# One decode step of attention and a feed-forward layer on one core: GpSimd issues the large loads in place of SP

## The chip, the cores and the metric

The kernel runs on one core of a Trainium2 chip. The metric is device time in microseconds. The engines are TensorE (PE), VectorE (DVE), ScalarE (ACT), GpSimd (POOL) and the sync engine (SP); transfers between HBM and the on-chip memory run on 16 DMA engines, whichever engine issues them.

## What is computed

One token's row x of 512 values is normalised; the result xn goes through grouped-query attention over a cache of 65536 positions (8 key heads, 4 query heads on each, 128 values a head) and through a feed-forward layer, and x and both are added.

```python
def _A_ref(x, k_cache, v_cache, wq, wo):
    q = (x @ wq) ...                        # 32 heads of 128
    scores = jnp.einsum("bhqd,bhkd->bhqk", q, k) * (Dh ** -0.5)
    p = _softmax(scores, axis=-1)
    o = jnp.einsum("bhqk,bhkd->bhqd", p, v)
    return o.reshape(B, Sq, Hq * Dh) @ wo   # heads brought together first
def _B_ref(x, w1, w2):
    return jnp.einsum("bsf,fd->bsd", jnp.maximum(x @ w1, 0), w2)   # 512 -> 1792 -> 512
xn = _layernorm(x, axis=-1)
return x + _A_ref(xn, ...) + _B_ref(xn, ...)
```

All data is float32. Keys and values are 268 MB each; wq and wo are 8.4 MB each, w1 and w2 3.7 MB each.

## The kernel before

The work is a chain of 34 turns on PE with the same code: a turn multiplies what lies in the key buffer kt by the current query columns (line 313). Turn 0 finds wq there and makes the queries; turns 1 to 32 find a chunk of keys (4 chunks of 16384 positions for each of 8 heads); the last finds wo. There is one key buffer kt and one value buffer vt, of 128 rows x 64 KB each; a chunk fills one. wt holds w1 and later w2.

Around a chunk: DVE transposes the scores (366) and finds the maximum (384 to 391). ACT takes the exponentials (254, 256); its first instruction also releases kt through the semaphore kfree. PE multiplies the probabilities by vt (292), and releases vt through vfree (299). `take(engine, semaphore, n)` waits until the semaphore has n and takes n off it. A transfer that lands raises its semaphore by 16: k or v for the chunks, on which PE waits.

SP issues all large transfers in one order: three pieces of wq into kt, w1 into wt, then in a loop values n on vfree and keys n+1 on kfree (lines 161 to 170), then wo in three pieces into kt, and, when the hidden row hT is there, w2 in five pieces into wt, and the store. ACT issues two loads of x (234, 235).

GpSimd prepares constants, finishes the norm (208 to 214), waits for w1 and multiplies it by xn and adds its four parts (219 to 224, whose end raises the semaphore sum); PE's line 281 sums that over the partitions, in every turn anew. GpSimd then waits until the last turn for the transposed row and makes hT (226). At the end PE adds w2's blocks (331, 339) as they land.

Of the kernel before, what the change touches and what calls it, by code (L numbers as in the profile page):

```python
# [13 lines left out]
D = 512  # L14
# [21 lines left out]
NCH = SK // CHUNK  # L36
# [6 lines left out]
WO_CUTS = [16, 8, 8]  # L43
W2_CUTS = [6, 4, 2, 1, 1]
# [5 lines left out]
def take(e, sem, n=1):  # L50

    return e.sem_inc(sem, -n).wait_op(sem, n, "sem-ge")  # L52


def starts(cuts):
    return [sum(cuts[:i]) for i in range(len(cuts) + 1)]

# [2 lines left out]
def attention_and_mlp_kernel(  # L60
# [12 lines left out]
    sp, pe, dve, act, pool = nc.sync, nc.tensor, nc.vector, nc.scalar, nc.gpsimd  # L73
    scale = float(DH) ** -0.5

    def sbuf(name, *shape):
        return nc.alloc_sbuf_tensor(name, list(shape), F32).ap()
# [3 lines left out]
    def sem(name):  # L81
        if name not in sems:
            sems[name] = nc.alloc_semaphore(name)
        return sems[name]

    def after(ins, name, n=1):

        return ins.wait_op(sem(name), n, "sem-ge")

    kt = sbuf("kt", P, CHUNK)  # L90
    vt = sbuf("vt", P, CHUNK)
    wt = sbuf("wt", P, FB * D)
# [20 lines left out]
    hT = sbuf("hT", P, FB)  # L113
# [25 lines left out]
    wo_row = wo[0].rearrange("d j n -> d (j n)")  # L139
    w1_row = w1.rearrange("p a f -> p (a f)")  # L140
    w2_row = w2.rearrange("p b n -> p (b n)")
    v_row = v[0].rearrange("(n p b) d -> n p (b d)", p=P, b=NB)
    wq_at, wo_at, w2_at = starts(WQ_CUTS), starts(WO_CUTS), starts(W2_CUTS)

    def of_own_row(cols, groups):
# [11 lines left out]
    for i in range(1, len(WQ_CUTS)):  # L157
        cut = slice(wq_at[i], wq_at[i + 1])
        sp.dma_start(kt[:, cut], wq_row[:, cut]).then_inc(sem(WQ_SEMS[i]), 16)  # L159
    sp.dma_start(wt, w1_row).then_inc(sem("w1"), 16)  # L160
    take(sp, sem("kfree"))
    sp.dma_start(kt, k[0, 0]).then_inc(sem("k"), 16)
    with sp.Fori(0, NCH - 1) as n:
        take(sp, sem("vfree"))
        sp.dma_start(vt, v_row[bass.ds(n, 1)].rearrange("o p n -> (o p) n")).then_inc(sem("v"), 16)
        take(sp, sem("kfree"))
        sp.dma_start(kt, k[0, bass.ds(n + 1, 1)].rearrange("o p n -> (o p) n")).then_inc(sem("k"), 16)
    take(sp, sem("vfree"))
    sp.dma_start(vt, v_row[NCH - 1]).then_inc(sem("v"), 16)
    take(sp, sem("kfree"))  # L170
    for i in range(len(WO_CUTS)):
        cut = slice(wo_at[i] * D, wo_at[i + 1] * D)
        sp.dma_start(kt[:, cut], wo_row[:, cut]).then_inc(sem(f"wo{i}" if i else "k"), 16)
    sp.wait_ge(sem("hT"), 1)
    for i in range(len(W2_CUTS)):
        cut = slice(w2_at[i] * D, w2_at[i + 1] * D)
        sp.dma_start(wt[:, cut], w2_row[:, cut]).then_inc(sem(f"w2{i}"), 16)  # L177
    sp.wait_ge(sem("y"), 1)
    sp.dma_start(out.rearrange("(p a) -> p a", p=P), ysb[:, 0, :]).then_inc(sem("ends"), 16)

# [3 lines left out]
    def link(ins):  # L184

        if chain[0]:
            after(ins, "pool", chain[0])
        chain[0] += 1
        return ins.then_inc(sem("pool"), 1)
# [22 lines left out]
    link(pool.tensor_scalar_mul(xn, xc, st[:, 7:8]))  # L212
    take(pool, sem("ends"), 16)
    after(pool.tensor_copy(qpad[:, :XA], xn), "pool", chain[0]).then_inc(sem("q"), 1)
    f = DFF_ALL
    w1_of = [wt[:, a * f : (a + 1) * f] for a in range(XA)]
    pool.wait_ge(sem("w1"), 16)
# [2 lines left out]
    last.then_inc(sem("pool"), 1)  # L220
    chain[0] += 1
    after(pool.tensor_add(w1_of[0], w1_of[0], w1_of[1]), "pool", chain[0])  # L222
    link(pool.tensor_add(w1_of[2], w1_of[2], w1_of[3]))  # L223
    after(pool.tensor_add(w1_of[0], w1_of[0], w1_of[2]), "pool", chain[0]).then_inc(sem("sum"), 1)  # L224
    hbig = ysum[:, : FB * 32].rearrange("p (b i) -> p b i", i=32)
    after(pool.tensor_scalar_max(hT, hbig[:, :, 0], 0.0), "hx").then_inc(sem("hT"), 1)  # L226


    def next_of(ins):
# [41 lines left out]
    with nc.body("turns", valid_engines=[pe.engine]):  # L271
# [3 lines left out]
        with pe.If(t > 1):  # L275
# [12 lines left out]
            n = NB // WIDE  # L288
# [167 lines left out]
```

## Time and profile before

| | us |
|---|---|
| median of 3 runs | 1303.71 |
| lowest and highest run | 1303.10 and 1303.74 |
| profiled execution: span from its first to its last instruction | 1301.3 |
| PE busy (matmul) | 774.9 |
| DVE busy | 274.8 |
| ACT busy | 76.2 |
| GpSimd busy | 34.8 |

Of the profiled execution the profile gives the span and no other time; the runs' median lies 2.4 us above it, which is taken for what lies around the span. The profile shows one execution. In its lines L313 is line 313 of the kernel, "kt<-k" is a tile written from a tensor, x31 a count. PEq, SPq and so on are the sequencers that issue. A transfer's time to landing runs from its issue to the semaphore. The timeline puts several like instructions of an engine together in one line, with the start of the first and their time in all, and behind them in brackets how long the engine was idle before.

### The profile page before, as it was taken

How to read it: one execution, taken by the hardware profiler on the slowest of the kernel's cores; microseconds unless marked ns; L12 is line 12 of the kernel's file. 1: busy time of each engine (PE TensorE's matmuls, PEld its weight loads, DVE VectorE, ACT ScalarE, POOL GpSimd, SP SyncE). 2: the span in 40 equal slices, each digit the busy share in tenths (PEclk: the TensorE clock that was granted, in tenths of full speed). 3: DMA queues.
4: the chain of work that ended last, by engine and by line, in shares of the span. 5: the costliest groups of instructions: out<-in, count | busy, mean ns of one | idle time of the engine just before them, and what ended most of it. 6: DMA issues, size and time to landing. Idle time of an engine off the chain costs nothing.

```text
span 1301.3 us, 13055 instructions
## 1 busy us (share of the span) xinstructions
PE 774.9 (60%) x5474; PEld 231.1 (18%) x5474; DVE 274.8 (21%) x466; ACT 76.2 (6%) x299; POOL 34.8 (3%) x30
## 2 busy tenths in 40 slices
PE   3365674665576456566555566666567466557557
PEld 1111121111121111121111121111112111112112
DVE  2211222211222220222220122221122221122222
ACT  1000000000000000000000000000000000000000
POOL 1900000000000000000000000000000000000000
PEclk9677877776887777786776777677777777777779
DMA  9999999999999999999999999999999999999998
GB/s 403 451 419 451 419 451 419 435 435 419 451 419 451 419 451 419 449 421 423 447 419 451 419 451 419 451 419 435 435 419 451 419 451 419 451 419 443 427 420 370
DMA packets 11236, 561.02 MB, mean 431 GB/s; under 512 B 1505, under 2 KB 1505, under 8 KB 1890
## 3 DMA queue, kind: packets, MB, share of 16 engines
q1 hardware_dynamic: 11088, 561.00, 99.7%
q10 hardware_dynamic: 146, 0.00, 0.0%
q8 instruction: 1, 0.02, 0.0%
q14 instruction: 1, 0.01, 0.0%
HBM read 560.99 MB, written 0.00 MB: 431 GB/s over the span
## 4 chain that ended last, share of the span: by engine, by line
issue 94%; DMA 3%; POOL 2%; SPq 0%; PE 0%; DVE 0%; POOLq 0%
DMA wt<-w 3%; POOL wt L219 1%; POOL wt L224 0%; POOL wt L222 0%; POOL wt L223 0%; SPq L177 0%; SPq L159 0%; PE banks L339 0%; DVE ysb L417 0%; SPq L151 0%; POOL hT L226 0%; SPq L452 0%; POOLq L156 0%
## 5 line engine op out<-in xcount | busy, mean ns | idle before, releaser
L313 PE MATMUL banks<-kt,qpad 128*32 128x512 f32 x2176 | 310.0, 733 | 311.1 <-PEq L52 308.7
L292 PE MATMUL banks<-vt,probs 128*16 128x512 f32 x2048 | 271.3, 690 | 82.1 <-PEq L52 82.1
L366 DVE STREAM_TRANSPOSE tr<-banks 128x1024 f32<-128x1024 f32 x136 | 170.0, 1250 | 471.4 <-PE banks L313 466.8
L313 PEld LDWEIGHTS banks<-kt,qpad 128*32 128x32 f32 x2176 | 84.5, 131 | 509.6 <-issue 496.3
L281 PE MATMUL banks<-wt,ones 128*1 128x448 f32 x768 | 121.3, 786 | 0.0
L292 PEld LDWEIGHTS banks<-vt,probs 128*16 128x16 f32 x2048 | 68.4, 108 | 298.4 <-issue 298.4
L392 DVE COPY o_sb<-banks 128x512 f32<-128x512 f32 x32 | 22.1, 692 | 455.3 <-PE banks L292 455.3
L254 ACT ACTIVATE corr<-diff 128x8 f32<-128x8 f32 x32 | 6.7, 208 | 1179.8 <-ACTq L52 1179.8
L256 ACT ACTIVATE probs<-tr,nb_new 128x128 f32<-128x128 f32 x128 | 65.3, 521 | 0.0
L276 PE MATMUL banks<-ident,m 128*4 128x128 f32 x32 | 9.7, 303 | 78.9 <-DVE m L384 78.9
L302 PE MATMUL banks<-sel,o_sb 128*128 128x4 f32 x256 | 32.8, 252 | 18.7 <-PEq L52 18.7
L302 PEld LDWEIGHTS banks<-sel,o_sb 128*128 128x128 f32 x256 | 31.0, 191 | 20.6 <-issue 20.6
L226 POOL TENSOR_SCALAR hT<-ysum 128x14 f32<-128x14 f32 x1 | 0.3, 257 | 1220.7 <-DVE ysum L404 1220.7
L384 DVE TENSOR_REDUCE m<-tr 128x4 f32<-128x512 f32 x32 | 32.2, 1006 | 2.9
L281 PEld LDWEIGHTS banks<-wt,ones 128*1 128x1 f32 x768 | 20.2, 100 | 58.9 <-issue 58.4
L277 PE MATMUL banks<-dg,ones 4*128 4x4 f32 x64 | 15.4, 309 | 20.0 <-DVE dg L387 20.0
L256 ACT ACTIVATION_READ_ACCUMULATOR probs<-tr,nb_new 128x1 f32 x128 | 24.0, 187 | 0.0
L276 PEld LDWEIGHTS banks<-ident,m 128*4 128x4 f32 x32 | 2.6, 81 | 108.0 <-DVE m L384 108.0
L219 POOL TENSOR_SCALAR wt<-wt,xn 128x1792 f32<-128x1792 f32 x4 | 19.1, 4797 | 16.5 <-DMA wt<-w 16.5
L277 PEld LDWEIGHTS banks<-dg,ones 4*128 4x128 f32 x64 | 12.6, 245 | 27.1 <-DVE dg L387 27.1
L299 PEld LDWEIGHTS banks<-part_sum,ones 128*128 128x128 f32 x64 | 9.5, 188 | 27.2 <-issue 27.2
L395 DVE TENSOR_TENSOR lo_run<-lo_run,banks 128x8 f32<-128x8 f32 x32 | 5.2, 163 | 40.0 <-DVEq L52 40.0
(69 smaller groups left out, 91.1 us busy)
## 6 DMA issues: line engine op xcount, KB each, us to landing
kt<-wq SPq DMA_DIRECT2D x2, 2048.0 KB, 9.3
kt<-wq SPq DMA_DIRECT2D x1, 4096.0 KB, 20.8
kt<-wo SPq DMA_DIRECT2D x1, 4096.0 KB, 15.5
kt<-wo SPq DMA_DIRECT2D x2, 2048.0 KB, 22.2
wt<-w SPq DMA_DIRECT2D x1, 3584.0 KB, 28.9
wt<-w SPq DMA_DIRECT2D x1, 1536.0 KB, 9.5
wt<-w SPq DMA_DIRECT2D x1, 1024.0 KB, 11.7
kt<-k SPq DMA_DIRECT2D x32, 24.1
```

Source lines behind the costliest of these rows:

```text
L219: last = pool.tensor_scalar_mul(w1_of[a], w1_of[a], xn[:, a : a + 1])
L256: last = act.activation(probs[:, :, g], tr[:, :, g], AF.Exp, bias=nb_new[:, g : g + 1], scale=scale, accum_out=part_sum[:, g : g + 1],)
L276: after(pe.transpose(pma[:GROUP, :P], m, ident), "d2p").then_inc(sem("p2d"), 1)
L277: after(pe.matmul(pmb[:, :GROUP], ones[:GROUP, :], dg, start=True, stop=True), "d2p", 2).then_inc(sem("p2d"), 1)
L281: ins = pe.matmul(hrow[32 * c : 32 * c + 1, :], ones[:, :1], hb[:, :, 32 * c : 32 * c + 32], start=True, stop=True,)
L292: last = pe.matmul(acc[c : c + WIDE * GROUP, :], probs[:, b : b + WIDE, :].rearrange("p b g -> p (b g)"), vt[:, b * DH : (b + WIDE) * DH], ...
L299: pe.matmul(lo_new[:, 0, :], ones, part_sum, start=True, stop=True).then_inc(sem("vfree"), 1)
L302: last = pe.matmul(lo_new[:, 1, :], o_sb[:, b, :], sel[:, b, :], start=(b == 0), stop=(b == WIDE - 1),)
L313: last = pe.matmul(pair[s // 2 % 2][32 * c : 32 * c + 32, s % 2 * 512 : s % 2 * 512 + 512], qpad, kb[:, s * 16 : s * 16 + 16, c, :], start ...
L366: ins = after(dve.transpose(tr2[:, s * 1024 : (s + 1) * 1024], pair[s % 2]), "p2d", s + 1)
L384: dve.reduce_max(m, tr.rearrange("p b i -> p i b")[:, :GROUP, :], axis=AX.X).then_inc(sem("d2p"), 1)
L392: after(dve.tensor_copy(o_sb.rearrange("p b d -> p (b d)"), acc), "p2d", 7).then_inc(sem("d2p"), 1)
```

## The change

GpSimd issues the keys, the values, wo and w2. Keys 0 and values 0 stand ahead of its wait for w1, the rest behind its work on w1. These transfers raise new semaphores, k_in, v_in and wo0; SP, which keeps wq, w1 and the store, waits for each in turn and raises k or v by 16 in its place. wo1, wo2 and w2's semaphores are raised by the transfers themselves, as before. Each transfer is asked for with one packet for each of its 128 rows. GpSimd's loop over the chunks is written out.

```diff
+def relay_of(sem):
+    def relay(e, to, of, n):
+        e.sem_inc(sem(to), 16).wait_op(sem(of), n, "sem-ge")
+    return relay
...
     sp.dma_start(wt, w1_row).then_inc(sem("w1"), 16)
-    take(sp, sem("kfree"))
-    sp.dma_start(kt, k[0, 0]).then_inc(sem("k"), 16)
-    with sp.Fori(0, NCH - 1) as n:
-        take(sp, sem("vfree"))
-        sp.dma_start(vt, v_row[bass.ds(n, 1)].rearrange("o p n -> (o p) n")).then_inc(sem("v"), 16)
-        take(sp, sem("kfree"))
-        sp.dma_start(kt, k[0, bass.ds(n + 1, 1)].rearrange("o p n -> (o p) n")).then_inc(sem("k"), 16)
-    take(sp, sem("vfree"))
-    sp.dma_start(vt, v_row[NCH - 1]).then_inc(sem("v"), 16)
-    take(sp, sem("kfree"))
-    for i in range(len(WO_CUTS)):
-        cut = slice(wo_at[i] * D, wo_at[i + 1] * D)
-        sp.dma_start(kt[:, cut], wo_row[:, cut]).then_inc(sem(f"wo{i}" if i else "k"), 16)
-    sp.wait_ge(sem("hT"), 1)
-    for i in range(len(W2_CUTS)):
-        cut = slice(w2_at[i] * D, w2_at[i + 1] * D)
-        sp.dma_start(wt[:, cut], w2_row[:, cut]).then_inc(sem(f"w2{i}"), 16)
+    for n in range(NCH):
+        relay(sp, "k", "k_in", 16 * (n + 1))
+        relay(sp, "v", "v_in", 16 * (n + 1))
+    relay(sp, "k", "wo0", 16)
     sp.wait_ge(sem("y"), 1)
...
     after(pool.tensor_copy(qpad[:, :XA], xn), "pool", chain[0]).then_inc(sem("q"), 1)
+    def load_keys(n, **how):
+        take(pool, sem("kfree"))
+        pool.dma_start(kt, k[0, n], **how).then_inc(sem("k_in"), 16)
+    def load_values(n):
+        take(pool, sem("vfree"))
+        pool.dma_start(vt, v_row[n]).then_inc(sem("v_in"), 16)
+    load_keys(0)
+    load_values(0)
     f = DFF_ALL
...
     after(pool.tensor_add(w1_of[0], w1_of[0], w1_of[2]), "pool", chain[0]).then_inc(sem("sum"), 1)
+    for n in range(1, NCH):
+        load_keys(n)
+        load_values(n)
+    take(pool, sem("kfree"))
+    for i in range(len(WO_CUTS)):
+        ...
+        pool.dma_start(kt[:, cut], wo_row[:, cut]).then_inc(sem(f"wo{i}"), 16)
     hbig = ysum[:, : FB * 32].rearrange("p (b i) -> p b i", i=32)
     after(pool.tensor_scalar_max(hT, hbig[:, :, 0], 0.0), "hx").then_inc(sem("hT"), 1)
+    pool.wait_ge(sem("hT"), 1)
+    for i in range(len(W2_CUTS)):
+        ...
+        pool.dma_start(wt[:, cut], w2_row[:, cut]).then_inc(sem(f"w2{i}"), 16)
```

Two places on the engines show what it moves. The first is GpSimd between the copy of the query columns and its work on w1 (wt holds w1). Before:

```order
L214 COPY qpad<-xn 128x4 [waits ends,pool]
L219 TENSOR_SCALAR wt<-wt,xn 128x1792 [waits w1]
L219 TENSOR_SCALAR wt<-wt,xn 128x1792 x3
L222 TENSOR_TENSOR wt<-wt 128x1792 [waits pool]
L223 TENSOR_TENSOR wt<-wt 128x1792 [waits pool]
L224 TENSOR_TENSOR wt<-wt 128x1792 [waits pool]
L226 TENSOR_SCALAR hT<-ysum 128x14 [waits hx]
```

And with the change:

```order
L211 COPY qpad<-xn 128x4 [waits ends,pool]
L214 DMA kt<-k 128x16384 [waits kfree]
L218 DMA vt<-v 128x16384 [waits vfree]
L226 TENSOR_SCALAR wt<-wt,xn 128x1792 [waits w1]
L226 TENSOR_SCALAR wt<-wt,xn 128x1792 x3
L229 TENSOR_TENSOR wt<-wt 128x1792 [waits pool]
L230 TENSOR_TENSOR wt<-wt 128x1792 [waits pool]
L231 TENSOR_TENSOR wt<-wt 128x1792 [waits pool]
L214 DMA kt<-k 128x16384 [waits kfree]
```

Keys 0 and values 0 stand ahead of the work on w1, keys 1 and all that follows behind it.

The second is the end. Before, SP issued what follows the last values, and hT stood alone on GpSimd:

```order
L169 DMA vt<-v 128x16384 [waits vfree]
L173 DMA kt<-wo 128x8192 [waits kfree]
L173 DMA kt<-wo 128x4096 x2
L177 DMA wt<-w 128x3072 [waits hT]
L177 DMA wt<-w 128x2048
L177 DMA wt<-w 128x1024
L177 DMA wt<-w 128x512 x2
L179 DMA y<-ysb 128x4 [waits y]
```

With the change the same stands on GpSimd, with the making of hT in between:

```order
L218 DMA vt<-v 128x16384 [waits vfree]
L238 DMA kt<-wo 128x8192 [waits kfree]
L238 DMA kt<-wo 128x4096 x2
L240 TENSOR_SCALAR hT<-ysum 128x14 [waits hx]
L244 DMA wt<-w 128x3072 [waits hT]
L244 DMA wt<-w 128x2048
L244 DMA wt<-w 128x1024
L244 DMA wt<-w 128x512 x2
```

The store alone stays on SP, behind the 65 relays.

More of the change, by code (lines that the diff above doesn't have):

```diff
@@ L88, in after @@
         return ins.wait_op(sem(name), n, "sem-ge")
+    relay = relay_of(sem)
     kt = sbuf("kt", P, CHUNK)
@@ L224, in attention_and_mlp_kernel @@
     after(pool.tensor_add(w1_of[0], w1_of[0], w1_of[2]), "pool", chain[0]).then_inc(sem("sum"), 1)
+    for n in range(1, NCH):
[3 more added lines that the diff above has]
+    for i in range(len(WO_CUTS)):
+        cut = slice(wo_at[i] * D, wo_at[i + 1] * D)
+        pool.dma_start(kt[:, cut], wo_row[:, cut]).then_inc(sem(f"wo{i}"), 16)
     hbig = ysum[:, : FB * 32].rearrange("p (b i) -> p b i", i=32)
     after(pool.tensor_scalar_max(hT, hbig[:, :, 0], 0.0), "hx").then_inc(sem("hT"), 1)
+    pool.wait_ge(sem("hT"), 1)
+    for i in range(len(W2_CUTS)):
+        cut = slice(w2_at[i] * D, w2_at[i + 1] * D)
+        pool.dma_start(wt[:, cut], w2_row[:, cut]).then_inc(sem(f"w2{i}"), 16)
     def next_of(ins):
```

## The prediction

> **What bounds the kernel now.** I read the page first: its slices, its packet counts and its queues.
>
> ```profile
> span 1301.3 us, 13055 instructions
> DMA  9999999999999999999999999999999999999998
> DMA packets 11236, 561.02 MB, mean 431 GB/s; under 512 B 1505, under 2 KB 1505, under 8 KB 1890
> q1 hardware_dynamic: 11088, 561.00, 99.7%
> ```
>
> The DMA engines are busy from end to end, and nearly all bytes are on SP's queue q1. SP issues 77 transfers in the code (3 of wq, w1, 32 of keys, 32 of values, 3 of wo, 5 of w2, the store), each over 128 rows. 77 x (128 + 16) = 11088: so before, too, a row is one packet, of 64 KB for keys and values, and each transfer has 16 small packets that raise its semaphore. "One packet for each row" is therefore no fewer packets than now.
>
> Next, the windows (columns: busy time and count per engine, granted clock, DMA share, GB/s):
>
> ```profile
> 0.00:40.00 40.00, 9.98 (x68) 3.28 (x68) 9.34 (x9) 4.61 (x11) 12.35 (x24) 0.85 0.96 406
> 200.00:1200.00 1000.00, 610.42 (x4272) 180.91 (x4276) 208.24 (x359) 58.15 (x234) 0.00 (x0) 0.75 1.00 433
> 1270.00:1302.00 32.00, 22.89 (x200) 6.86 (x192) 9.19 (x16) 0.00 (x0) 0.26 (x1) 0.93 0.86 360
> ```
>
> In the long middle the DMA share is 1.00 at 433 GB/s. Only the first microseconds and the last 4 or so are not transfer time. PE at 61% and GpSimd at nothing have room. So the change can gain only if a byte becomes cheaper to move, and loses only if the engines run dry or a byte becomes dearer.
>
> The period comes from the timeline: first reads of a key chunk by PE, at chunk 1 and chunk 31.
>
> ```profile
> 89.22 0.23 PEld L313 LDWEIGHTS banks<-kt,qpad 128*32 128x32 f32 x8 [10.42 <-issue]
> 1250.43 0.23 PEld L313 LDWEIGHTS banks<-kt,qpad 128*32 128x32 f32 x8 [7.68 <-issue]
> ```
>
> (1250.43 - 89.22) / 30 = 38.71 us per pair of chunks, 19.35 us per 8.39 MB transfer, 2.42 us per row on each of 16 engines (8 rows each). How long a transfer waits behind the other one is read from its issue line:
>
> ```profile
> L167 SPq DMA_DIRECT2D kt<-k x31: 332/333/343, 65.5 to 1225.9; - x31
> DMA to landing us min/median/max: 23.5/24.1/25.3
> L165 SPq DMA_DIRECT2D vt<-v x31: 332/333/343, 27.2 to 1201.6; - x31
> DMA to landing us min/median/max: 28.4/29.3/42.6
> ```
>
> Keys are issued 24.1 - 19.35 = 4.75 us before the values ahead of them end (4.15 at the least), values 9.95 us (9.05 at the least) before the keys ahead of them end. These are the covers of the change: GpSimd may be that much slower to start a transfer before an engine runs dry.
>
> **The change part by part.** *Issue and relay in the loop.* 72 transfers move from SP (0.33 us each, off the path) to GpSimd, and 65 semaphore relays are put on SP, each between a landing and PE. A hop through SP is bounded by the way from ACT's release of the keys to SP's issue:
>
> ```profile
> 65.02 0.21 ACT L254 ACTIVATE corr<-diff 128x8 f32<-128x8 f32 x1 [50.54 <-ACTq L52]
> 65.47 0.34 SPq L167 DMA_DIRECT2D kt<-k  x1
> ```
>
> 65.47 - 65.23 = 0.24 us. It comes off the covers and adds nothing to the path while they hold. SP waits in the order in which chunks land, so no relay stands behind a later one; GpSimd's queue takes keys and values in the order of their releases, as SP's did. What GpSimd needs from release to first byte, L, the trace does not show. The nearest rows are transfers of 2 KB from SP and from ACT:
>
> ```profile
> xT<-x ACTq DMA_DIRECT2D x1, 2.0 KB, 8.2
> y<-ysb SPq DMA_DIRECT2D x1, 2.0 KB, 1.4
> ```
>
> 1.4 us on idle engines; 8.2 us where 2 KB went out beside wq's rows. L lies between; I take 2, close to the store's, since nothing but the transfer ahead stands in the way, and a further 1.9 us would still fit. With L = 2 and the relay, 4.15 - 2.24 leaves 1.9 us of cover at the least: term 0. [...]
>
> *The first pass.* Here the order on GpSimd matters (wt holds w1): keys 0 now come on another queue than w1, and keys 1 are issued behind seven GpSimd operations on w1. The chain of waits and the timeline give the times before:
>
> ```profile
> 2.22 28.86 DMA wt<-w
> 31.17 19.13 POOL wt L219 x4
> 58.39 3.99 POOL wt L224
> 26.46 0.33 SPq L162 DMA_DIRECT2D kt<-k  x1
> 69.88 0.16 PEld L292 LDWEIGHTS banks<-vt,probs 128*16 128x16 f32 x8 [2.56 <-issue]
> 64.23 4.66 PE L281 MATMUL banks<-wt,ones 128*1 128x448 f32 x24
> 77.53 0.33 SPq L165 DMA_DIRECT2D vt<-v  x1
> ```
>
> w1 lands at 31.08 and GpSimd is through at 62.38, 31.3 us later; values 0 land at about 69.8. Keys 0, released at 26.46, used to queue behind w1. On a queue of its own it shares the engines with w1's rest: the 8.2 us of xT above, issued while wq's first 2 MB was moving, are what alternation by packets gives; first in, first out over both queues would not. A w1 row (28 KB) takes 2.42 x 28/64 = 1.06 us. Keys 0 join at 26.46 + 2 = 28.5, with 2.6 us or 2 to 3 rows of w1 left on each engine, each of which now waits for one 64 KB row: w1 lands 4.8 to 7.3 us later. GpSimd is through at 67.2 to 69.7 and the first byte of keys 1 can come at 69.2 to 71.7, against the 69.8 at which the engines run out: 0 to 1.9 us lost, once. I take 0.7. The late sum also holds PE's line 281 (4.66 us), so that values 1 are released up to 4.7 us later, at 82.2; keys 1 land at about 89.9, so that is covered.
>
> *The end.* On GpSimd wo, hT and w2 now follow one another. Between hT and w2 no other engine is woken; before, SP waited for hT.
>
> ```profile
> 1263.90 1.29 SPq L173 DMA_DIRECT2D kt<-wo  x3
> 1269.79 0.18 PEld L292 LDWEIGHTS banks<-vt,probs 128*16 128x16 f32 x8 [4.99 <-issue]
> 1283.38 2.24 SPq L177 DMA_DIRECT2D wt<-w  x5
> 1289.33 1.25 DVE L366 STREAM_TRANSPOSE tr<-banks 128x1024 f32<-128x1024 f32 x1 [1.64 <-DMA kt<-wo]
> 1285.18 12.80 DMA wt<-w
> ```
>
> wo is issued 5.9 us before the last values land, w2 5.9 us before the last of wo: at L = 2 both still queue behind running transfers, and each later piece has the piece before it as cover. The last landing (1297.98) stays tied to the bytes: term 0.
>
> *A row's price.* wo's three transfers took 1289.33 - 1269.79 = 19.54 us, against 19.35 for the same bytes in one: 0.19 us for 18 more packets on each engine, some 10 ns a packet. GpSimd's packets are as many; I take them at the same price, and bound them by nothing and by twice that: 72 x 8 x 10 ns = 5.8 us either way.
>
> The sum: 1301.3 + 0.7 = 1302.0 us of span; the runs' median of 1303.7 is 2.4 us above the span, which I leave: 1304.4 us.
>
> **The rivals.** (A, slower) *Every key starts late.* If L + 0.24 exceeds the cover of 4.75 us, each pair waits for the rest, 31 times. At L = 5 that is 0.5 x 31 = 15.5 us: 1319; each further microsecond adds 31. It decides at L = 4.5 (the worst chunks from 3.9). For it: no row shows GpSimd starting a transfer, and xT's 8.2 us lies beyond the cover. Against it: the store's 1.4 us.
>
> (B, slower) *The change does not do what it says: GpSimd's rows of a transfer stay together.* Then w1's rest waits for all of keys 0 and lands near 50.4; GpSimd is through at 81.7, keys 1 begin at 83.7, 13.9 us after values 0 ended. Seven packets fewer in each of 72 transfers give 5.0 us back: +8.9, 1312.6. The rows on q1 (144 packets a transfer) speak against it, for another issuer. [...]
>
> (C, faster) *Row packets from GpSimd are cheaper*, by half of the 10 ns to all of it: -2.9 to -5.8, 1297.9 to 1300.8. No row shows GpSimd's packets; the 10 ns are all that a packet is seen to cost beyond its bytes, so there is no more to gain this way.
>
> (D, slower) *They are dearer*, by 10 ns: +5.8, 1309.5. [...]
>
> **How the numbers follow.** Forecast 0.58 (own range 1303.2 to 1306.0), A 0.13, B 0.07, C 0.13, D 0.09. About 0.2%, 2.6 us, is what a measurement here can tell from no change. Faster: C, 0.13. Same: the forecast but for 0.02 in which the first pass costs more: 0.56. Slower: 0.31. The range runs from C's better half to B, 1298.5 to 1313, and leaves out A but for its edge, the far end of C and a larger D: some 0.17.
>
> **What would show it.** Right: a DMA share of 1.00 at 433 GB/s between 200 and 1200 us; w1 landing at 36 to 38 and GpSimd's line 231 ending at 67 to 70; a notch below 2 us near 70 us; keys 0.2 to 2 us closer to the end of the values ahead. Wrong: a period of the pairs other than 38.71 us (A where slices between pairs fall, C or D where the share stays 1.00), far fewer packets on GpSimd's queue than 144 a transfer (B), or an end after the last w2 that grows.

## The result, and the profile after

The changed kernel takes 1316.41 us (median of four runs, 1315.95 to 1318.25) against 1303.4 us before: 1.0102 times as long, 95% interval 1.0088 to 1.0117. The forecast was 1304.4 us with a range of 1298.5 to 1313.0, and "same", which the prediction takes as less than 2.6 us; the kernel is 13.0 us slower.

The page of the changed kernel, in its head, its DMA totals and its queues (packets, MB, share of 16 engines' span):

```profile
span 1313.9 us, 12900 instructions
DMA packets 11110, 561.04 MB, mean 427 GB/s; under 512 B 1505, under 2 KB 1505, under 8 KB 1762
q0 software_dynamic: 10240, 548.93, 97.0%
```

The window view of the middle of the program (the last two columns are the DMA share and GB/s):

```profile
200.00:1200.00 1000.00, 603.70 (x4228) 178.82 (x4232) 208.22 (x359) 57.99 (x234) 26.90 (x51) 0.74 1.00 431
```

GpSimd's queue is q0. 72 transfers of 144 packets would be 10368; 128 fewer came, all of them from w2's last two pieces, whose 2 KB rows went out in pairs. The DMA share in the middle is 1.00 as before, but at 431 GB/s in place of 433: packets are in flight all the time, and some of them take longer. The end shows the rest. First the timeline from w2's issue on (three of its lines), and the line of the same store before the change:

```profile
1288.39 2.69 POOL L244 DMA_DIRECT2D wt<-w  x5 [0.30 <-POOL hT L240]
1296.22 1.25 DVE L384 STREAM_TRANSPOSE tr<-banks 128x1024 f32<-128x1024 f32 x1 [0.94 <-DMA kt<-wo]
1305.73 0.35 SPq L176 DMA_DIRECT2D y<-ysb  x1
```

```profile
1298.92 0.34 SPq L179 DMA_DIRECT2D y<-ysb  x1
```

Then the line view of the program's end (durations in ns, min/median/max), after and before:

```profile
L470 POOLq DRAIN  x3: 40/78/5946, 1307.2 to 1313.6; - x3
```

```profile
L452 POOLq DRAIN  x3: 34/46/64, 1300.4 to 1301.1; - x3
```

So the store is issued 1305.73 - 1298.92 = 6.81 us later, and behind it one DRAIN of GpSimd, an instruction of the program's closing lines, takes 5.95 us where none took more than 0.06; the other engines' last instructions stand behind its end. Together that is 12.7 us, against 1313.9 - 1301.3 = 12.6 us of span.

Where the 6.8 us arise is seen in the trace's packet records (start, length and size of each of the 8192 packets of 64 KB). The records do not name the engine; the 16 engines are told apart by which packet starts where another ends. Before, the packets take 2.42 us and 5 of them more than 2.5. After, the median is the same and 248 take 2.5 to 4.08 us. Some 160 of these are first rows of key transfers and some 40 are second rows, and they cost time where the keys were issued shortly before an engine came free ("out of step" is the time from the first engine that comes free to the last):

| kernel | keys 1 to 31: first engine free after the issue, least / median | engines out of step there, median | keys with under 2.8 us | lost in their packets | lost in the other keys' packets |
|---|---|---|---|---|---|
| before | 3.28 / 3.82 us | 0.38 us | 0 | 0 | 0.37 us |
| after | 1.09 / 2.80 us | 1.60 us | 16 | 4.93 us | 0.40 us |

("Lost" is what the packets took beyond 2.42 us, summed and divided by 16 engines.) Values, issued more than 5 us ahead, lose next to nothing in either kernel: 5 of their 4096 packets take over 2.5 us before, 31 after. The table accounts for 5.0 of the 6.8 us. By the same records the engines also stood empty between packets for 1.1 us more, on the mean of the 16, and at the end of the last values the last engine was 1.2 us behind the mean of all, where it was 0.3 before.

GpSimd is later than SP twice. Two lines of the changed kernel's timeline at one key's release:

```profile
1231.63 0.21 ACT L272 ACTIVATE corr<-diff 128x8 f32<-128x8 f32 x1 [35.94 <-ACTq L52]
1232.42 0.53 POOL L214 DMA_DIRECT2D kt<-k  x1 [25.19 <-POOLq L52]
```

1232.42 - 1231.84 = 0.58 us from ACT's release to the issue, against SP's 0.24; and from the issue to the first packet on an engine that is idle 1.23 us against 0.97 (packet records of the twin runs below). In all 0.6 us.

The first pass lost nothing:

```profile
31.15 19.12 POOL L226 TENSOR_SCALAR wt<-wt,xn 128x1792 f32<-128x1792 f32 x4 [2.81 <-DMA wt<-w]
58.40 3.99 POOL L231 TENSOR_TENSOR wt<-wt 128x1792 f32<-128x1792 f32 x1
65.10 0.59 POOL L214 DMA_DIRECT2D kt<-k  x1 [2.72 <-POOLq L52]
```

w1 landed where it had before (GpSimd's first operation on it starts at 31.15, before at 31.17), GpSimd was through at 62.39, and keys 1 were issued on their release, at 65.10 where it was 65.47.

### The profile page after: what moved, and what is told of

It reads as the page before. It is cut to its first block, busy times and chain, and to the rows that moved or that the text cites. A ratio compares the mean times of both kernels' runs of the same rounds, so it can differ in the third digit from the quotient of the medians.

```text
span 1313.9 us, 12900 instructions
## 1 busy us (share of the span) xinstructions
PE 775.9 (59%) x5474; PEld 231.3 (18%) x5474; DVE 274.8 (21%) x466; ACT 76.0 (6%) x299; POOL 73.2 (6%) x102
## 3 DMA queue, kind: packets, MB, share of 16 engines
q0 software_dynamic: 10240, 548.93, 97.0%
## 5 line engine op out<-in xcount | busy, mean ns | idle before, releaser
L310 PE MATMUL banks<-vt,probs 128*16 128x512 f32 x2048 | 267.1, 681 | 80.7 <-PEq L52 80.7
L214 POOL DMA_DIRECT2D kt<-k x32 | 17.2, 536 | 743.2 <-POOLq L52 743.2
L218 POOL DMA_DIRECT2D vt<-v x32 | 16.9, 529 | 421.6 <-POOLq L52 421.6
```

The lines of the kernel that those rows point to most:

```text
L214: pool.dma_start(kt, k[0, n], **how).then_inc(sem("k_in"), 16)
L218: pool.dma_start(vt, v_row[n]).then_inc(sem("v_in"), 16)
L310: last = pe.matmul(acc[c : c + WIDE * GROUP, :], probs[:, b : b + WIDE, :].rearrange("p b g -> p (b g)"), vt[:, b * DH : (b + WIDE) * DH], ...
```

## The experiments

Theory: the last DRAIN is paid for the transfers that GpSimd has issued, and the keys are late by GpSimd's slower start. Main rival: GpSimd's packets, or the use of its queue, are dearer in themselves. A second rival: the relays make the keys late.

**More cover for the keys, GpSimd issuing.** kt is released by DVE as soon as PE has read it, not by ACT.

```diff
-            turn_scores()
+            turn_scores(free="kfree")
-        act.activation(corr, ..., AF.Exp).then_inc(sem("kfree"), 1)
+        act.activation(corr, ..., AF.Exp)
```

> The changed kernel, but kt is released where PE has ended the last score matmul of a chunk (by DVE, ahead of the chunk's last transpose) instead of by ACT's first instruction, some 4.7 us earlier. Theory (late keys and a long last wait): GpSimd's keys reach the engines 2.4 us or more after their issue, and on the engine that is free first the cover is down to 1.2 to 4 us; with 4.7 us more no key is late, all 64 KB packets take 2.42 us again, the last w2 lands near 1298, the last wait of GpSimd stays at 5.9 us, and the time is near 1310. Rival (GpSimd's packets are dearer in themselves): nothing changes, 1316.

Measured: 1309.7 us (ratio 1.0048, 1.0032 to 1.0065). The window view of this run's middle, the store in its timeline, and its last DRAIN in the line view:

```profile
200.00:1200.00 1000.00, 601.17 (x4281) 179.97 (x4281) 208.21 (x359) 58.75 (x234) 26.91 (x51) 0.76 1.00 433
```

```profile
1299.37 0.35 SPq L176 DMA_DIRECT2D y<-ysb  x1
```

```profile
L470 POOLq DRAIN  x3: 40/77/5946, 1300.9 to 1307.3; - x3
```

With the first engine free at least 6.65 us after each issue no key is late (19 packets over 2.5 us), and the store goes out 0.45 us later than before the change. GpSimd's packets are as cheap as SP's: 433 GB/s in the middle, as before the change. What is left is the DRAIN.

**Control: the same release with SP issuing.** The same edit of the kernel before.

> The control: the kernel before with kt released early. Theory: no key was late before, so nothing changes, within 0.5 us of 1303.5. Rival (the early release is a gain in itself, which hid a cost of GpSimd's issue in the first experiment): 1 us or more faster.

Measured: 1303.49 us, ratio 1.0000 (0.999 to 1.001). The early release is worth nothing where no key is late; what it gave above, 6.7 us, is what the late keys had cost.

**The relay alone.** SP issues all; GpSimd passes the landings on.

```diff
-        sp.dma_start(vt, v_row[...]).then_inc(sem("v"), 16)
+        sp.dma_start(vt, v_row[n]).then_inc(sem("v_in"), 16)
+    for n in range(NCH):
+        relay(pool, "v", "v_in", 16 * (n + 1))
+        relay(pool, "k", "k_in", 16 * (n + 1))   # of keys n + 1
```

> The relay alone: SP issues everything as before (written out), landings of chunks raise new semaphores and GpSimd passes them on to PE (keys 0 go straight). Theory: a hop costs some 0.25 us and comes off the cover of the keys, which in the kernel before is 3.3 us on the engine that is free first; SP's first byte needs about 1 us, so 2 us are left: 1303.4 to 1304.5. Rival (it is the relays that make the keys late): 1306 to 1310 with no last wait on GpSimd.

Measured: 1303.82 us, ratio 1.0003 (0.9993 to 1.0012); 2 packets over 2.5 us, the first engine free 3.06 us after the issue at the least. A relay on GpSimd makes no key late; SP's 65 relays of the changed kernel are also in the first experiment, where no key is late. The relays are not the cause.

**GpSimd's and SP's start on empty engines.** In twin kernels the issuer waits for values n to land before it issues keys n + 1; in SP's, GpSimd passes the landings on to PE.

```diff
     for n in range(1, NCH):
+        pool.wait_ge(sem("v_in"), 16 * n)
         load_keys(n)
```

> The changed kernel with GpSimd waiting for values n-1 to land before it issues keys n, so that 31 keys start on empty engines and their issue to landing shows what GpSimd needs. Theory: issue to landing of a key is 19.35 plus 2.4 to 3.5 us, against SP's row in the twin run some 1.2 to 1.5 us less; the time grows by 31 times (that and the wake-up): 1390 to 1430. Rival (GpSimd starts as fast as SP, and something else made the keys late): both runs agree, near 1350.

> The twin: SP issues as in the kernel before (written out), waits for values n-1 to land before it issues keys n, and GpSimd passes the landings on to PE. Theory: issue to landing of a key 19.35 plus 1.2 to 1.6 us, and 1345 to 1360 in all. Rival: the same as with GpSimd.

Measured: 1412.94 and 1381.48 us. The keys' lines with their times to landing, from the line view, GpSimd as issuer first:

```profile
L214 POOL DMA_DIRECT2D kt<-k x32: 527/527/746, 27.2 to 1332.1; - x32
DMA to landing us min/median/max: 21.9/22.1/23.7
```

```profile
L178 SPq DMA_DIRECT2D kt<-k x31: 327/328/328, 69.8 to 1306.9; - x31
DMA to landing us min/median/max: 21.7/21.9/22.4
```

Against 19.35 us of transfer, a start from nothing takes 2.75 and 2.55 us. I had expected a difference of 1.2 us or more here; it is 0.2, as SP needs longer than thought too, and SP's run lies above the 1345 to 1360 expected. Without the DRAIN the runs differ by 1412.94 - 5.9 - 1381.48 = 25.6 us, 0.83 per key: most of GpSimd's delay lies ahead of its issue (one semaphore instruction of it is this experiment's own). The 2.75 us are the 2.8 us of the table: the 16 keys of the changed kernel that were issued later than that before an engine came free lost 4.93 us in their packets, the other 15 only 0.40. On the empty engines of both runs a key's first rows took 3.1 us in the median (packet records).

**SP made late.** The kernel before, with kt released by the first, the second or the third of ACT's four exponentials on a chunk, 0.5, 1.0 and 1.5 us later. GpSimd issues nothing. No run has the release at the fourth.

```diff
-        act.activation(corr, ..., AF.Exp).then_inc(sem("kfree"), 1)
+        act.activation(corr, ..., AF.Exp)
         for g in range(GROUP):
             last = act.activation(probs[:, :, g], ...)
+            if g == 1:        # 0 and 2 in the other two
+                last.then_inc(sem("kfree"), 1)
```

> The kernel before, SP issuing, kt released by the first of ACT's four exponentials: some 0.5 us later. In the profiles GpSimd's key issue starts 0.58 us after ACT's release against SP's 0.24, and its first packet 1.23 us after the issue against 0.97: 0.6 us later in all. Theory (start time alone): a loss at the last landing like the changed kernel's 5.5 us, somewhat less: 1305.5 to 1309. Rival (GpSimd's path makes its own late rows): 1303.0 to 1304.5, since half a microsecond fits.

> The kernel before, SP issuing everything, but kt is released by ACT's third instruction pair on a chunk (the second of four heads' exponentials) instead of by its first instruction, about 1.0 us later. That is what the twin runs and the relay say GpSimd takes longer from release to bytes (0.83 + 0.25 us). Theory (the late keys are a matter of start time alone): packets grow long at the head of key transfers and the engines get out of step as with GpSimd, 4 to 7 us, 1307.5 to 1310.5, with nothing added at the end. Rival (1 us still fits into the cover of 3.3 to 5.2 us, and GpSimd's path adds something of its own): 1303.0 to 1304.5.

> The same, released by the third exponential, some 1.5 us later: the dose after 0.5 and 1.0 us (1316.0). Theory: 1320 to 1340. Rival (the run at 1.0 us was a chance): below 1312.

| kernel | time, median (range) | ratio, interval | first engine free, least / median | keys under 2.8 us | lost in their packets |
|---|---|---|---|---|---|
| 0.5 us later | 1312.04 (1310.16 to 1319.61) | 1.0074, 1.0055 to 1.0093 | 0.24 / 2.13 us | 23 | 5.97 us |
| 1.0 us later | 1315.99 (1312.43 to 1321.03) | 1.0091, 1.0058 to 1.0125 | -0.37 / 1.80 us | 28 | 10.21 us |
| 1.5 us later | 1317.31 (1315.02 to 1321.87) | 1.0109, 1.0091 to 1.0127 | -0.39 / 1.85 us | 29 | 9.28 us |

A late start alone, with SP's own packets and nothing at the end, costs as much as GpSimd's 0.6 us did and more: 8.6 us for half a microsecond. The first two are slower than I expected (1305.5 to 1309, 1307.5 to 1310.5), the third is faster (1320 to 1340): the loss grows far less than the delay, 8.6, 12.6 and 13.9 us. The median spread of the engines points to what happens: 0.38 us before, 1.97, 2.10 and 1.47 here. A long first row (up to 4.08 us in the changed kernel, against 2.42) puts one engine behind the others; the next release waits for the last engine to land, the next transfer is wanted by the first; so a late key shortens the cover of the keys after it. In the changed kernel this can be followed: up to key 8 the engines are 0.6 to 0.8 us out of step and the first is free 2.8 us or more after each issue; from key 9 on they are 1.4 to 2.5 us out of step, and the cover falls to as little as 1.1. Runs of one kernel differ by up to 9.5 us. Why 0.5 us on SP costs somewhat more than 0.6 us on GpSimd (8.6 against 6.8) stays open.

**GpSimd for half of the chunks.** SP issues chunks 16 to 31, wo and w2.

```diff
-    for n in range(1, NCH):
+    for n in range(1, 16):
         load_keys(n)
         load_values(n)
```

> The changed kernel with GpSimd issuing only chunks 0 to 15 (32 transfers); SP issues chunks 16 to 31, wo and w2 itself, straight to the old semaphores. Theory: GpSimd's last wait is paid per transfer that it has issued, 5.95 / 72 = 0.083 us each, whenever they were: 2.6 us; the late keys of the first 16 chunks cost some 2 us: near 1308. Rival 1 (the wait is a fixed price of using GpSimd's queue): 5.9 us left, near 1311. Rival 2 (it is paid only for transfers that landed shortly before): 0.05 us, near 1305.5.

Measured: 1312.26 us (ratio 1.0069, 1.0052 to 1.0086). The end in the line view:

```profile
L477 POOLq DRAIN  x3: 40/78/2679, 1306.5 to 1309.6; - x3
```

2679 / 32 = 84 ns a transfer, against 5946 / 72 = 83: it is paid per transfer, however long ago. The time is 4 us more than forecast: all the 64 KB packets together lose 5.4 us here, nearly as much as the 6.3 us with all chunks (0.6 before the change), and some of SP's own keys in the second half were late, since the engines stayed 1.5 us out of step after GpSimd had stopped.

**Both causes taken away.** Half of the chunks, early release, and a DRAIN of GpSimd while SP issues.

```diff
-    for n in range(1, NCH):
+    for n in range(1, 16):
         ...
+    pool.drain()
```

> Both causes taken away, with the change's issue kept for 16 chunks: kt is released early as in the first experiment, GpSimd issues chunks 0 to 15 only, then drains its queue while SP issues the rest. Theory: no key is late, and GpSimd's last drain has nothing left (0.05 us in place of the 2.68 us of the run with half of the chunks): last landing as in the kernel before and 1303.4 to 1304.5 in all. Rival (a use of GpSimd's queue has a fixed price or dearer packets): 1306 or more.

Measured: 1305.01 us (ratio 1.0012, 1.0003 to 1.0022). GpSimd's own DRAIN and the one at the end, in the line view:

```profile
L250 POOLq DRAIN  x1: 36582/36582/36582, 623.3 to 623.3; - x1
L478 POOLq DRAIN  x3: 34/41/78, 1302.9 to 1303.3; - x3
```

The DRAIN can be had early: it waited 36.6 us for the last transfers while nobody waited for GpSimd, and 0.04 us are left at the end. 1.7 us remain, 0.5 more than I allowed. The packet records show some 1.0 us of them at the handover, where keys 16 on SP's queue shared the engines with values 15 and values 16 then came 1.27 us ahead of a free engine, and most of the rest in the first 100 us.

**Joined rows.** The first experiment with `single_packet=True` on keys 1 to 31 and all values.

> The first experiment (early release) with the rows of one transfer joined to one packet on each engine, for keys 1 to 31 and all values. Theory: a packet costs some 8 to 10 ns beyond its bytes, 7 fewer in each of 63 transfers: 3.5 to 4.4 us off the last landing against 1309.7, 1305.3 to 1306.2; the last wait of GpSimd stays 5.9 us if it is paid per transfer, and falls below 2 us if it is paid per packet (then 1301 to 1302).

Measured: 1309.83 us, the same as 1309.7 without it. GpSimd's queue on this run's page, and the line view of the end:

```profile
q0 software_dynamic: 10240, 548.93, 97.1%
```

```profile
L470 POOLq DRAIN  x3: 40/78/5946, 1300.9 to 1307.2; - x3
```

Neither the records (10240, 2.42 us a row) nor the time know a difference: the rows were not joined. The 10 ns a row are not saved by asking for one packet; that expectation was wrong, and what joined rows would cost stays open.

**Twice as many key transfers over the same rows.** The first experiment, each key chunk in two transfers of 64 rows.

```diff
-        pool.dma_start(kt, k[0, n], **how).then_inc(sem("k_in"), 16)
+        for r in (0, P // 2):
+            pool.dma_start(kt[r : r + P // 2], k[0, n][r : r + P // 2], **how).then_inc(sem("k_in"), 16)
```

> The first experiment (early release) with each key chunk loaded by two GpSimd transfers of 64 rows in place of one of 128: 104 transfers in place of 72 over the same rows. GpSimd's last drain: 104 x 0.083 = 8.6 us if it is paid per transfer, 5.9 us if it is paid per row.

Measured: 2096.63 us (one run). The keys among the page's DMA issues (count, median us to landing), and the line view of the end:

```profile
kt<-k POOLq DMA_DIRECT2D x64, 41.3
```

```profile
L471 POOLq DRAIN  x3: 40/78/8559, 2085.6 to 2094.6; - x3
```

8559 / 104 = 82 ns: per transfer, not per row. The time itself was a surprise, told at the end.

## Why the prediction was wrong

- **The end: missed.** "The runs' median of 1303.7 is 2.4 us above the span, which I leave", and the program's end inside the span was left as it was too. It holds a DRAIN of GpSimd, which took 0.06 us at most before; it now takes 5.95 us, 0.083 for each of 72 transfers. No rival had it; only the list of signs had "an end after the last w2 that grows".
- **Issue and relay in the loop: term 0, measured 6.8 us.** The mechanism, a late start, was named in rival A; the step that failed is the comparison of cover and start. The cover was taken from the semaphore, that is from the last engine (4.15 us at the least); the engine that is free first had 3.28. Against it stood L, the time to the first byte, taken as 2. As such it was near: 0.58 + 1.23 = 1.8 us. But a transfer was not at full speed with its first byte (first rows of 3.1 us on empty engines, against 2.42); from release to full speed GpSimd needed 0.58 + 2.75 = 3.3 us, SP 0.24 + 2.55 = 2.8. And the cover was treated as a threshold for each key by itself ("it decides at L = 4.5", "each further microsecond adds 31"), while a late key puts the engines out of step and shortens the next cover, so that 0.6 us were enough for half of the keys to be late, each of those 16 losing 0.3 us on the mean.
- **The relay: right.** 0.24 us were allowed; alone, on GpSimd, it costs nothing measurable.
- **The first pass: 0.7, measured 0.** w1's last rows were not delayed. The step that failed is that each of w1's last rows would wait for a row of keys. Keys 0 were issued at 27.05, so that a first packet could have come at 28.28 (1.23 us later); then 1 to 2 rows of w1 had yet to start on each engine, and these went first. The first packet of keys began at 30.36, as w1's rows ended. Why they went first no run shows.
- **A row's price: right at 0 either way.** With cover enough, the packets take 2.42 us from either issuer (over 2.5 us: 19 of 8192 in the first experiment, 5 before the change), so C and D fall. B falls as w1 was not held up (31.15 against 31.17) and GpSimd's queue holds a record for each row but w2's last (10240 in all); that joined rows would hold w1's rest up was its assumption, which no run shows. Where values 15 on GpSimd's queue met keys 16 on SP's (the run with both causes taken away), all 16 engines took rows from the two queues in turn.
- **The order at the end of the program (wo, hT, w2 on GpSimd): right.** w2 was issued 7.8 us before wo's last landing and nothing ran dry.

That both undone causes bring the time back to within 1.7 us, and that a late SP alone reproduces the second, is shown. The self-feeding of late keys is argued from the packet records; no run took the spread alone away.

## What to carry to other kernels

Where transfers follow one another without a gap, read the cover of each from its buffer's release to the first engine that comes free, not to the landing, and hold it against the whole way from the release to full speed (3.3 us with GpSimd, 2.8 with SP here). Half a microsecond too late on each of 31 keys cost 8.6 us here, with the engines out of step. Before loads are moved to GpSimd, count them: each cost 83 ns at the end here unless GpSimd drained earlier, and if they must move, release the buffer where the last reader ends.

## What the runs showed of the hardware that was not expected

- GpSimd's DRAIN cost 82 to 84 ns for every transfer that it had issued since its last one: 32, 72 and 104 transfers gave 2.68, 5.95 and 8.56 us, and 0.04 were left where it had drained before.
- The 16 engines, once out of step, stayed so for long: with GpSimd stopped after half of the chunks, they were still some 1.5 us apart through the other half.
- Two loads of 64 rows in place of one of 128 took the kernel from 1309.7 to 2096.6 us; a 64 KB packet then takes 4.6 us in the median in place of 2.42, and 3196 of the 8192 take over 5 us. Why they take nearly twice the time no run here shows.
